# A six-layer cross network on one core: first rows and last blocks transposed on TensorE, first weights issued by ScalarE, last block finished in pieces

## The chip, the cores and the metric

The kernel runs on one core of one Trainium2 chip. The metric is device time in microseconds (us): the median of timed runs. Beside it stands one profiled execution, whose trace the profile is made from.

## The reference

A cross network: `x0` is 16384 x 1024, there are 6 layers with a 1024 x 1024 weight each, all in bfloat16.

```python
x = x0
for l in range(6):
    proj = jnp.einsum('bd,de->be', x, ws[l]) + bs[l]
    x = x0 * proj + x
return x
```

## The kernel before

**Tiling.** The 16384 rows are worked in 16 pairs (`pr`) of two blocks of 512 rows. All activations are held transposed: features on the 128 partitions, rows along the free dimension. `x0T[:, n, k, :]` is block n, feature group k of 8. Each layer of a pair is a 1024 x 1024 by 1024 x 1024 product, done as a seven-product (Strassen-like) scheme on 512 x 512 blocks: `pid` 1 to 7, each of 16 matmuls of 128 x 128 by 512 columns (`mm`, L241). In pairs 1 to 15 product 2 is split once more into smaller products of 256 columns (`inner`, L247). Products 1, 2 and 4 use blocks of the layer's weight as they are (W11, W21, W22); 5, 6, 7, 3 and 8 use combinations.

**Pair 0** also makes the combinations: `emit_combo` adds and subtracts weight blocks on VectorE (DVE), and `flush_saves` stores them in a scratch tensor `Lc` in HBM, from which pairs 1 to 15 load them. The first combination is product 5's, `w12 + W22`. The differences of activations (`T1` to `T4`, `Ops.t`) are made on DVE too; T1 needs both blocks of x0.

**After the matmuls** ScalarE (ACT) moves PSUM to SBUF with the bias (`abias`, L47) or without (`acopy`, L44), and DVE sums, multiplies by x0 (`f_mul`) and adds x (`f_add`). Both engines' operations are pinned to the order in which they are written (`pin`); TensorE's are not.

**Queues.** All DMAs are issued by SyncE (SP; its queue is written SPq), one after another. The weight ring `wring` holds 12 tiles of 512 KB; `prefetch_upto` issues loads ahead. At the start SP issues, in this order: W11 (L176), a DMA transpose of x0's rows 0 to 511 (L180), W21 (L182), a DMA transpose of rows 512 to 1023 (L184), W12 (L116, through `load_w12`), a DMA transpose of the biases (L187, cast to float on GpSimd at L190), W22 (L93), and then layer 1's loads.

**Between pairs** (shown for pair 0 to 1): the result `xst` is transposed back by one DMA transpose (L421) into `x0T`'s memory, stored (L424), and behind these stand the next loads from `Lc` (L93) and the transposes of the next x0 rows (L408).

**The last pair** has its result in four regions (feature half eh, block n). Each `f_add` of the last layer writes `xfin`, `out_region` issues a DMA transpose of that region (L210), and all four stores (L415) are kept behind the last of the transposes by `nosync`.

Of the kernel before, what the change touches and what calls it, by code (L numbers as in the profile page):

```python
# [6 lines left out]

ADD = mybir.AluOpType.add
SUB = mybir.AluOpType.subtract
# [7 lines left out]
def kernel(  # L17
# [22 lines left out]
    def vtt(out, in0, in1, op):  # L40
        return pin(nc.vector.tensor_tensor(out=out, in0=in0, in1=in1, op=op))  # L41
# [28 lines left out]
    def w_src(l, pid):  # L70
        wl = ws[l]
        if pid == 1:
            return wl[0:H, 0:H].rearrange("(k p) e -> p k e", p=P)
        if pid == 2:
            return wl[H:D, 0:H].rearrange("(k p) e -> p k e", p=P)
        if pid == 4:
            return wl[H:D, H:D].rearrange("(k p) e -> p k e", p=P)
        return Lc[l, CIDX[pid]].rearrange("p (k e) -> p k e", k=KH)
# [33 lines left out]
    def load_w12(l):  # L112
        st = combo_st.setdefault(l, {})
        if "w12" not in st:
            st["w12"] = w12_pool.tile([P, KH, H], BF16, name="w12")
            state["last_dma"] = nc.sync.dma_start(st["w12"][:], ws[l][0:H, H:D].rearrange("(k p) e -> p k e", p=P))  # L116
        return st["w12"]
# [54 lines left out]
            B, T = self.B, self.T  # L172
            return {1: B[0, 0], 2: B[1, 0], 3: B[1, 1]}[pid] if pid <= 3 else T[{4: 4, 5: 1, 6: 2, 7: 3}[pid]][:]

    wt0 = wring.tile([P, KH, H], BF16, name="wp")
    nc.sync.dma_start(wt0[:], w_src(0, 1))  # L176
    wtiles[(0, 0, 1)] = wt0
    x0T_next = x0t_pool.tile([P, 2, KD, NB], BF16, name="x0T")
    LK = L * KD
    nc.sync.dma_start_transpose(out=x0T_next[:, 0], in_=x0[0:NB, :])  # L180
    wt2 = wring.tile([P, KH, H], BF16, name="wp")
    nc.sync.dma_start(wt2[:], w_src(0, 2))  # L182
    wtiles[(0, 0, 2)] = wt2
    nc.sync.dma_start_transpose(out=x0T_next[:, 1], in_=x0[NB:2 * NB, :])  # L184
    load_w12(0)
    b_bf = const.tile([P, LK], BF16, name="b_bf")
    nc.sync.dma_start_transpose(out=b_bf[:], in_=bs.rearrange("l (m p) -> (l m) p", p=P))  # L187
    b_all = const.tile([P, LK], FP32, name="b_all")
    prefetch_upto(7)
    nc.gpsimd.tensor_copy(b_all[:], b_bf[:])  # L190
    ops = Ops(x0T_next, 0, False)
    ops.t(1)
    for pid in (5, 6, 3):
        emit_combo(0, pid)
    ops.t(2)
    emit_combo(0, 7)
    prefetch_upto(PREF)
    flush_saves()

    step = 0  # L200
    for pr in range(NPAIR):
        x0T = x0T_next
        xst = xst_pool.tile([P, 2, KD, NB], BF16, name="xst")
        last_pair = pr == NPAIR - 1
        xo_last = {"t": None, "regions": [], "tins": [], "xfin": None}

        def out_region(eh, n):
            if xo_last["t"] is None:
                xo_last["t"] = xo_pool.tile([P, 2, 2, KH, KH, P], BF16, name="xoS")
            ti_ = nc.sync.dma_start_transpose(out=xo_last["t"][:, eh, n].rearrange("p j k r -> p (j k) r"),  # L210
                                              in_=xo_last["xfin"][:, eh, n].rearrange("r j k p -> r (j k p)"))
            xo_last["regions"].append((eh, n))
            xo_last["tins"].append(ti_)

        for l in range(L):
            last_layer = l == L - 1
# [42 lines left out]
            def bank():  # L259
                return psX.tile([P, NB], FP32, name="px")  # L260
# [11 lines left out]
            def f_add(Cb, eh, r):  # L272
                n = r ^ flip
                c, xs = Cb[:, :, r, :], xsrc[:, n, eh * KH:(eh + 1) * KH, :]
                if last_pair and last_layer:
                    if xo_last["xfin"] is None:
                        xo_last["xfin"] = xst_pool.tile([P, 2, 2, KH, KH, P], BF16, name="xst")
                    v4 = lambda a: a.rearrange("r k (j p) -> r k j p", p=P)
                    vtt(xo_last["xfin"][:, eh, n].rearrange("r j k p -> r k j p"), v4(c), v4(xs), ADD)
                    out_region(eh, n)  # L280
                else:
                    vtt(xst[:, n, eh * KH:(eh + 1) * KH, :], c, xs, ADD)

# [3 lines left out]
            if small:  # L287
                w2i = weights(8)
                wi = w2i[:].rearrange("p k (j e) -> p k j e", e=HE)
                b = cur.rhs(2)  # L290
                ti = cur.ti
                EA = ei_pool.tile([P, KH, NB], BF16, name="ea")
                EB = ei_pool.tile([P, KH, NB], BF16, name="eb")
                c11, c12 = (slice(0, 2), slice(0, NQ)), (slice(0, 2), slice(NQ, NB))
                c21, c22 = (slice(2, 4), slice(0, NQ)), (slice(2, 4), slice(NQ, NB))
                q2, q5, q1 = bank(), bank(), bank()
                for m in range(3):
                    mm(1, w1, pA, m, True)
                    ev(P1s, pA, m, 0)
                inner(q1, w2[:, 0:2, 0:HE], b[:, 0:2, 0:NQ], True)  # L300
                evi(EA[:, c11[0], c11[1]], q1)
                inner(q5, wi[:, 0], ti[:, 0], True)
                evi(EB[:, c22[0], c22[1]], q5)
                mm(1, w1, pA, 3, True)
                ev(P1s, pA, 3, 0)
                inner(q2, w2[:, 2:4, 0:HE], b[:, 2:4, 0:NQ], True)
                evi(EB[:, c11[0], c11[1]], q2)
                pX = [bank() for _ in range(KH)]
                w5 = weights(5)
                mm(5, w5, pX, 0, True)  # L310
# [12 lines left out]
                evi(EA[:, c21[0], c21[1]], q1)  # L323
                w3 = weights(3)
                mm(3, w3, pX, 0, False)
                ev(S53, pX, 0, 0)
                mm(5, w5, pX, 3, True)
                ev(P5s, pX, 3)
                for m in range(1, KH):
                    mm(3, w3, pX, m, False)  # L330
                    ev(S53, pX, m, 0)
                half_sum(EA, EA, EB, 0)
                cur.t(3)
                vtt(EA[:, c22[0], c22[1]], EA[:, c22[0], c22[1]], EB[:, c22[0], c22[1]], ADD)
                cur.t(4)
                vtt(C1[:, :, 0, :], P1s[:], EA[:], ADD)
            else:
                P2s = evt()
                for m in range(KH):
                    mm(1, w1, pA, m, True)  # L340
                    ev(P1s, pA, m, 0)
                pX2 = [bank() for _ in range(KH)]
                for m in range(KH):
                    mm(2, w2, pX2, m, True)
                    ev(P2s, pX2, m)
                pX = [bank() for _ in range(KH)]
                w5 = weights(5)
                for m in range(KH):
                    mm(5, w5, pX, m, True)
                    ev(P5s, pX, m)  # L350
                w3 = weights(3)
                for m in range(KH):
                    mm(3, w3, pX, m, False)
                    ev(S53, pX, m, 0)
                cur.t(3)
                cur.t(4)
                vtt(C1[:, :, 0, :], P1s[:], P2s[:], ADD)
# [30 lines left out]
            if more:  # L388
                ops.inner_t((1,))
                ops.t(1)  # L390
                ops.inner_t((2, 3, 4))
            f_mul(C2, 1, 0)
            f_add(C2, 1, 0)
            if more:
                ops.t(2)
            if combos_next:
                emit_combo(l + 1, 7)
                emit_combo(l, 8)
                if l + 1 == L - 1:
                    stage_ctx.close()  # L400
                    xo_pool = ctx.enter_context(tc.tile_pool(name="xo", bufs=1))
            elif pr == 0:
                emit_combo(l, 8)
# [6 lines left out]
                        nosync(ti_, state["last_dma"], "keep the x0 prefetch behind the already issued weight loads")  # L410

        if last_pair:
            for (eh, n) in xo_last["regions"]:
                r0 = pr * PR + n * NB
                si = nc.sync.dma_start(out[r0:r0 + NB, eh * H:(eh + 1) * H].rearrange("(j p) d -> p j d", p=P),  # L415
                                       xo_last["t"][:, eh, n].rearrange("p j k r -> p j (k r)"))
                for ti_ in xo_last["tins"]:
                    nosync(si, ti_, "stores after all output transposes")
            continue
        xo = x0T[:].rearrange("p n k (j r) -> p (n k j) r", r=P)  # L420
        nc.sync.dma_start_transpose(out=xo, in_=xst[:].rearrange("r n k b -> r (n k b)"))  # L421
# [34 lines left out]
```

## Time and profile before

| | us |
|---|---|
| median of 3 runs | 2329.14 (2328.7 to 2329.48) |
| profiled execution, its own time | 2331.35 |
| its span, first to last instruction | 2329.6 |
| TensorE matmul busy in the span | 2295.6 (99%) |
| DVE busy | 1988.8 (85%) |
| ACT busy | 1824.4 (78%) |

Matmuls are pipelined and their busy time overlaps, so 99% does not mean that TensorE is at its peak. Lines such as L241 are lines of the kernel before. The changed kernel's lines are shifted: L41, L44 and L47 become L42, L45 and L48, L93, L107 and L116 become L94, L108 and L117, and L241 and L247 become L281 and L287.

### The profile page before, as it was taken

What the parts mean: (1) busy time and instruction counts of PE and PEld (TensorE: products, weight loads), DVE (VectorE), ACT (ScalarE), POOL (GpSimd) and SP (SyncE); (2) the same over time, 40 slices, a digit from 0 to 9 for tenths busy, and PEclk for the clock granted to TensorE, in tenths of its full rate; (3) what the DMA queues carried; (4) which work ended last, traced back from release to release, by engine and by line L of the source; (5) the groups of instructions that cost most, each with busy time, mean ns of one, the idle gap of its engine ahead of it and who ended that gap; (6) DMA issues with size and microseconds to landing.
All of it is one profiled execution on the core that took longest, in us unless ns stands there. A gap on an engine that the chain in (4) does not pass through costs nothing.

```text
span 2329.6 us, 31728 instructions
## 1 busy us (share of the span) xinstructions
PE 2295.6 (99%) x11832; PEld 1158.5 (50%) x11832; DVE 1988.8 (85%) x2220; ACT 1824.4 (78%) x2959; POOL 0.4 (0%) x5
## 2 busy tenths in 40 slices
PE   7999999999999999999999999999999999999997
PEld 3444454555545454555555454555555454545553
DVE  6997888888888888888888888888888888888886
ACT  4776787878878787878778787878878787878786
POOL 0000000000000000000000000000000000000000
PEclk9999999999999999999999999999999999999999
DMA  8759578595875958669596785957859588595854
GB/s 235 229 178 303 185 200 261 172 289 172 209 258 176 287 172 221 240 189 272 186 244 216 194 266 180 262 202 196 268 173 283 177 203 262 171 295 170 238 189 109
DMA packets 613833, 508.56 MB, mean 218 GB/s; under 512 B 399664, under 2 KB 552240, under 8 KB 613680
## 3 DMA queue, kind: packets, MB, share of 16 engines
q1 hardware_dynamic: 613680, 506.53, 73.6%
q8 instruction: 94, 1.54, 0.3%
q14 instruction: 59, 0.48, 0.1%
HBM read 390.07 MB, written 49.28 MB: 189 GB/s over the span
## 4 chain that ended last, share of the span: by engine, by line
PE 96%; DVE 2%; SPq 1%; DMA 1%; issue 0%; ACT 0%; DVEq 0%
PE px L241 84%; PE px L247 12%; DVE cb L41 1%; DVE wp L41 1%; DVE xst L41 0%; DMA wp<-Lc 0%; SPq L180 0%; DVE T L41 0%; DMA wp<-in_ws_dram 0%; SPq L184 0%; SPq L187 0%; ACT cb L47 0%; SPq L116 0%; SPq L182 0%; SPq L176 0%
## 5 line engine op out<-in xcount | busy, mean ns | idle before, releaser
L241 PEld LDWEIGHTS <-wp 128*128 128x128 bf16 x9312 | 911.9, 98 | 1022.7 <-issue 14.0
L241 PE MATMUL px<-T,wp 128*128 128x512 bf16 x6144 | 1405.0, 380 | 3.3 <-DVE wp L41 3.3
L47 ACT ACTIVATE ev<-px,b_all 128x512 bf16<-128x512 f32 x1152 | 791.3, 687 | 225.6 <-PE px L241 212.0
L241 PE MATMUL px<-xst,wp 128*128 128x512 bf16 x2640 | 620.9, 379 | 0.4 <-DVE xst L41 0.4
L44 ACT CAST ev<-px 128x512 bf16<-128x512 f32 x792 | 463.3, 585 | 179.1 <-PE px L241 166.8
L41 DVE TENSOR_TENSOR cb<-cb,x0T 128x2048 bf16<-128x2048 bf16 x384 | 469.7, 1223 | 10.0
L41 DVE TENSOR_TENSOR cb<-ev 128x1024 bf16<-128x1024 bf16 (+1 forms) x390 | 263.1, 696 | 232.1 <-ACT ev L44 232.1
L41 DVE TENSOR_TENSOR xst<-cb,xst 128x2048 bf16<-128x2048 bf16 x320 | 392.0, 1225 | 22.4 <-PE px L241 0.5
L47 ACT ACTIVATE cb<-px,b_all 128x512 bf16<-128x512 f32 x384 | 263.6, 687 | 67.9 <-PE px L241 54.8
L247 PEld LDWEIGHTS <-wp 128*128 128x128 bf16 x2520 | 246.7, 98 | 133.2 <-DMA wp<-Lc 5.4
L247 PE MATMUL px<-ti,wp 128*128 128x256 bf16 x1440 | 216.7, 273 | 5.0 <-DMA wp<-Lc 5.0
L44 ACT CAST ea<-px 128x512 bf16<-128x512 f32 x360 | 211.7, 588 | 0.0
L41 DVE TENSOR_TENSOR T<-xst,T 128x2048 bf16<-128x2048 bf16 x160 | 195.5, 1222 | 8.3
L41 DVE TENSOR_TENSOR T<-xst 128x2048 bf16<-128x2048 bf16 x160 | 194.9, 1218 | 0.0
L44 ACT CAST eb<-px 128x512 bf16<-128x512 f32 x270 | 160.2, 593 | 6.1 <-PE px L247 6.1
L241 PE MATMUL px<-x0T,wp 128*128 128x512 bf16 x528 | 126.5, 385 | 10.5 <-DMA x0T<-in_x_dram 10.5
L247 PE MATMUL px<-xst,wp 128*128 128x256 bf16 x900 | 136.1, 274 | 0.0
L41 DVE TENSOR_TENSOR ea<-ea,eb 128x1024 bf16<-128x1024 bf16 (+1 forms) x180 | 99.9, 555 | 28.6 <-ACT eb L44 28.6
L41 DVE TENSOR_TENSOR cb<-ev,ea 128x2048 bf16<-128x2048 bf16 x90 | 109.7, 1218 | 0.0
L41 DVE TENSOR_TENSOR xst<-cb,x0T 128x2048 bf16<-128x2048 bf16 x64 | 78.4, 1225 | 2.2
L41 DVE TENSOR_TENSOR ti<-xst 128x512 bf16<-128x512 bf16 x150 | 63.2, 422 | 4.0 <-PE px L241 0.5
L41 DVE TENSOR_TENSOR ti<-xst,ti 128x512 bf16<-128x512 bf16 x150 | 62.7, 418 | 0.0
(14 smaller groups left out, 170.4 us busy)
## 6 DMA issues: line engine op xcount, KB each, us to landing
wp<-Lc SPq DMA_DIRECT2D x450, 512.0 KB, 3.9
wp<-in_ws_dram SPq DMA_DIRECT2D x288, 512.0 KB, 4.6
out_dram<-x0T SPq DMA_DIRECT2D x30, 1024.0 KB, 9.9
Lc<-wp SPq DMA_DIRECT2D x30, 512.0 KB, 3.3
w<-in_ws_dram SPq DMA_DIRECT2D x6, 512.0 KB, 5.1
out_dram<-xoS SPq DMA_DIRECT2D x4, 512.0 KB, 4.8
x0T<-in_x_dram SPq DMA_TRANSPOSE x32, 7.8
x0T<-xst SPq DMA_TRANSPOSE x15, 12.2
```

Source lines behind the costliest of these rows:

```text
L41: return pin(nc.vector.tensor_tensor(out=out, in0=in0, in1=in1, op=op))
L44: return pin(nc.scalar.copy(out=out, in_=in_))
L47: return pin(nc.scalar.activation(out=out, in_=in_, func=IDENT, bias=bias, scale=1.0))
L241: nc.tensor.matmul(pts[m][:], lhsT=wt[:, k, m * P:(m + 1) * P], rhs=rhs[:, k, :], start=(start and k == 0), stop=(k == KH - 1), **kw)
L247: nc.tensor.matmul(pt[:, m * NQ:(m + 1) * NQ], lhsT=w[:, k, m * P:(m + 1) * P], rhs=rhs[:, k, :], start=(start and m == 0 and k == 0), sto ...
```

## The change

- **Start.** The DMA transpose of rows 0 to 511 is replaced: SP loads the rows as they lie, in two halves of the features (`xrows`), and TensorE transposes them, 128 x 128 at a time, by a matmul against an identity matrix (`transpose_rows`), four into one PSUM bank; ACT and DVE copy the banks in turn to `x0T`. The first half is transposed before product 1, the second after product 1's first column group. The identity is made on GpSimd (a memset, in the built program a reload of the code library, and a select). DVE's T1, the first combinations and their saves are emitted after the second half.
- The biases are loaded as rows and transposed by one matmul instead of a DMA transpose and a GpSimd cast.
- The four raw blocks of layer 0's weight are issued by ACT's queue, one of SP's DMAs standing between the others. SP's order becomes: first half of x0's rows, biases, second half, DMA transpose of rows 512 to 1023, layer 1's loads.
- Eight matmuls on zeros run on TensorE before the first transpose, and a one-column copy on ACT.
- **End.** Of the last pair's four regions the two of the first feature half (eh = 0) keep the DMA transpose, but each is stored at once. The two of the second half are transposed by TensorE (`out_pe`), copied out of PSUM by ACT, or by ACT and DVE in turn, and stored in two pieces each. The very last block's multiply and add on DVE are cut into parts of 2, 1 and 1 of its four feature groups. TensorE takes the last block's transposes part by part.
- Pairs 1 to 14, and the order of all instructions between start and end on ACT, DVE and SP, are as before.

```diff
+    zero = const.tile([P, NB], BF16, name="zero")
+    nc.vector.memset(zero[:], 0.0)
+    ident = const.tile([P, P], BF16, name="ident")
+    make_identity(nc, ident[:])
...
-    nc.sync.dma_start_transpose(out=x0T_next[:, 0], in_=x0[0:NB, :])
...
+    xrows = [ev_pool.tile([P, KH, NB], BF16, name="ev") for _ in range(2)]
+    raw = {i: wring.tile([P, KH, H], BF16, name="wp") for i in (1, 2, 4)}
+    combo_st[0] = {"w12": w12_pool.tile([P, KH, H], BF16, name="w12")}
+    for h in range(2):
+        pin(nc.sync.dma_start(xrows[h][:], x0[0:NB, h * H:(h + 1) * H].rearrange("(r p) d -> p r d", p=P)))
+        if h == 0:
+            pin(nc.scalar.dma_start(raw[1][:], w_src(0, 1)))
+            pin(nc.sync.dma_start(b_rows[:], bs.rearrange("l (m p) -> (l m) p", p=P)))
+    pin(nc.scalar.dma_start(raw[2][:], w_src(0, 2)))
+    pin(nc.sync.dma_start_transpose(out=x0T_next[:, 1], in_=x0[NB:2 * NB, :]))
+    pin(nc.scalar.dma_start(combo_st[0]["w12"][:], ws[0][0:H, H:D].rearrange("(k p) e -> p k e", p=P)))
+    pin(nc.scalar.dma_start(raw[4][:], w_src(0, 4)))
...
+    acopy(warm_in[:], zero[:, 0:1])
+    warm = ps[1].tile([P, NB], FP32, name="px")
+    for _ in range(8):
+        nc.tensor.matmul(warm[:], lhsT=zero[:, 0:P], rhs=zero[:], start=True, stop=True)
+
+    def transpose_rows(h):
+        for k in range(KH):
+            pt = ps[1].tile([P, NB], FP32, name="px")
+            for r in range(KH):
+                nc.tensor.matmul(pt[:, r * P:(r + 1) * P], lhsT=xrows[h][:, r, k * P:(k + 1) * P], rhs=ident[:],
+                                 start=(r == 0), stop=True, skip_group_check=True)
+            dst = x0T_next[:, 0, h * KH + k, :]
+            if k % 2 == 0:
+                acopy(dst, pt[:])
+            else:
+                pin(nc.vector.tensor_copy(out=dst, in_=pt[:]))
+
+    transpose_rows(0)
+    pb = ps[1].tile([P, NB], FP32, name="px")
+    nc.tensor.matmul(pb[:, 0:LK], lhsT=b_rows[:], rhs=ident[0:LK, 0:LK], start=True, stop=True)
+    pin(nc.vector.tensor_copy(out=b_all[:], in_=pb[:, 0:LK]))
...
+        def out_region(n):
...
+            pin(nc.sync.dma_start_transpose(out=xo_last["t"][:, n].rearrange("p j k r -> p (j k) r"),
+                                            in_=xo_last["xfin"][:, n].rearrange("r j k p -> r (j k p)")))
+            r0 = pr * PR + n * NB
+            pin(nc.sync.dma_start(out[r0:r0 + NB, 0:H].rearrange("(j p) d -> p j d", p=P),
+                                  xo_last["t"][:, n].rearrange("p j k r -> p j (k r)")))
+
+        def out_pe(pts, n, ms, yo):
+            for j in range(KH):
+                for m in ms:
+                    nc.tensor.matmul(pts[j][:, m * P:(m + 1) * P], lhsT=xst[:, n, KH + m, j * P:(j + 1) * P], rhs=ident[:],
+                                     start=(m == 0), stop=True, skip_group_check=True)
+                if ms[-1] != KH - 1:
+                    continue
+                if len(ms) == KH or j % 2 == 1:
+                    acopy(yo[:, j, :], pts[j][:])
+                else:
+                    pin(nc.vector.tensor_copy(out=yo[:, j, :], in_=pts[j][:]))
+                if j % 2 == 1:
+                    r0 = pr * PR + n * NB + (j - 1) * P
+                    pin(nc.sync.dma_start(out[r0:r0 + 2 * P, H:D].rearrange("(j p) d -> p j d", p=P), yo[:, j - 1:j + 1, :]))
...
                 for m in range(KH):
                     mm(1, w1, pA, m, True)
                     ev(P1s, pA, m, 0)
+                    if step == 1 and m == 0:
+                        transpose_rows(1)
+                        ops.t(1)
+                        for pid in (5, 6, 3):
+                            emit_combo(0, pid)
+                        ops.t(2)
+                        emit_combo(0, 7)
+                        flush_saves()
...
-            f_mul(C2, 1, 0)
-            f_add(C2, 1, 0)
             if more:
+                f_mul(C2, 1, 0)
+                f_add(C2, 1, 0)
                 ops.t(2)
+            else:
+                n1, n0 = 1 ^ flip, flip
+                pT = [bank() for _ in range(KH)]
+                out_pe(pT, n1, range(KH), evt())
...
+                parts = [slice(0, 2), slice(2, 3), slice(3, 4)]
+                vtt(c(parts[0]), c(parts[0]), xz(parts[0]), MULT)
+                vtt(c(parts[1]), c(parts[1]), xz(parts[1]), MULT)
+                vtt(xs(parts[0]), c(parts[0]), xs(parts[0]), ADD)
+                vtt(c(parts[2]), c(parts[2]), xz(parts[2]), MULT)
+                vtt(xs(parts[1]), c(parts[1]), xs(parts[1]), ADD)
+                vtt(xs(parts[2]), c(parts[2]), xs(parts[2]), ADD)
+                pT2 = [psA.tile([P, NB], FP32, name="px") for _ in range(KH)]
+                yo = evt()
+                out_pe(pT2, n0, (0, 1, 2), yo)
+                out_pe(pT2, n0, (3,), yo)
...
-                for ti_ in xo_last["tins"]:
-                    nosync(si, ti_, "stores after all output transposes")
```

More of the change, by code (lines that the diff above doesn't have):

```diff
@@ L6 @@
 from concourse._compat import with_exitstack
+from concourse.masks import make_identity
 ADD = mybir.AluOpType.add
@@ L173, in rhs @@
             return {1: B[0, 0], 2: B[1, 0], 3: B[1, 1]}[pid] if pid <= 3 else T[{4: 4, 5: 1, 6: 2, 7: 3}[pid]][:]
-    wt0 = wring.tile([P, KH, H], BF16, name="wp")
-    nc.sync.dma_start(wt0[:], w_src(0, 1))
-    wtiles[(0, 0, 1)] = wt0
-    x0T_next = x0t_pool.tile([P, 2, KD, NB], BF16, name="x0T")
[L179 to L188, printed above, removed]
+    LK = L * KD
+    zero = const.tile([P, NB], BF16, name="zero")
+    nc.vector.memset(zero[:], 0.0)
+    ident = const.tile([P, P], BF16, name="ident")
+    make_identity(nc, ident[:])
+    b_rows = const.tile([LK, P], BF16, name="b_rows")
@@ new lines @@
+    b_all = const.tile([P, LK], FP32, name="b_all")
+    x0T_next = x0t_pool.tile([P, 2, KD, NB], BF16, name="x0T")
+    xrows = [ev_pool.tile([P, KH, NB], BF16, name="ev") for _ in range(2)]
[6 more added lines that the diff above has]
+            pin(nc.sync.dma_start(b_rows[:], bs.rearrange("l (m p) -> (l m) p", p=P)))
@@ new lines @@
+    pin(nc.scalar.dma_start(raw[2][:], w_src(0, 2)))
+    pin(nc.sync.dma_start_transpose(out=x0T_next[:, 1], in_=x0[NB:2 * NB, :]))
+    pin(nc.scalar.dma_start(combo_st[0]["w12"][:], ws[0][0:H, H:D].rearrange("(k p) e -> p k e", p=P)))
+    pin(nc.scalar.dma_start(raw[4][:], w_src(0, 4)))
+    for i in raw:
+        wtiles[(0, 0, i)] = raw[i]
+    warm_in = const.tile([P, 1], BF16, name="warm_in")
+    acopy(warm_in[:], zero[:, 0:1])
+    warm = ps[1].tile([P, NB], FP32, name="px")
+    for _ in range(8):
+        nc.tensor.matmul(warm[:], lhsT=zero[:, 0:P], rhs=zero[:], start=True, stop=True)
@@ L189 @@
+    transpose_rows(0)
+    pb = ps[1].tile([P, NB], FP32, name="px")
+    nc.tensor.matmul(pb[:, 0:LK], lhsT=b_rows[:], rhs=ident[0:LK, 0:LK], start=True, stop=True)
+    pin(nc.vector.tensor_copy(out=b_all[:], in_=pb[:, 0:LK]))
     prefetch_upto(7)
-    nc.gpsimd.tensor_copy(b_all[:], b_bf[:])
     ops = Ops(x0T_next, 0, False)
[L192 to L196, printed above, removed]
     prefetch_upto(PREF)
-    flush_saves()
     step = 0
@@ L204 @@
         last_pair = pr == NPAIR - 1
-        xo_last = {"t": None, "regions": [], "tins": [], "xfin": None}
-        def out_region(eh, n):
+        xo_last = {"t": None, "xfin": None}
+        def out_region(n):
             if xo_last["t"] is None:
[L209 to L213, printed above, removed]
+                xo_last["t"] = xo_pool.tile([P, 2, KH, KH, P], BF16, name="xoS")
+            pin(nc.sync.dma_start_transpose(out=xo_last["t"][:, n].rearrange("p j k r -> p (j k) r"),
[17 more added lines that the diff above has]
+                    pin(nc.sync.dma_start(out[r0:r0 + 2 * P, H:D].rearrange("(j p) d -> p j d", p=P), yo[:, j - 1:j + 1, :]))
         for l in range(L):
@@ L274, in f_add @@
                 c, xs = Cb[:, :, r, :], xsrc[:, n, eh * KH:(eh + 1) * KH, :]
-                if last_pair and last_layer:
+                if last_pair and last_layer and eh == 0:
                     if xo_last["xfin"] is None:
-                        xo_last["xfin"] = xst_pool.tile([P, 2, 2, KH, KH, P], BF16, name="xst")
+                        xo_last["xfin"] = xst_pool.tile([P, 2, KH, KH, P], BF16, name="xst")
                     v4 = lambda a: a.rearrange("r k (j p) -> r k j p", p=P)
-                    vtt(xo_last["xfin"][:, eh, n].rearrange("r j k p -> r k j p"), v4(c), v4(xs), ADD)
-                    out_region(eh, n)
+                    vtt(xo_last["xfin"][:, n].rearrange("r j k p -> r k j p"), v4(c), v4(xs), ADD)
+                    out_region(n)
                 else:
@@ L391 @@
                 ops.inner_t((2, 3, 4))
-            f_mul(C2, 1, 0)
-            f_add(C2, 1, 0)
             if more:
+                f_mul(C2, 1, 0)
+                f_add(C2, 1, 0)
                 ops.t(2)
+            else:
+                n1, n0 = 1 ^ flip, flip
+                pT = [bank() for _ in range(KH)]
+                out_pe(pT, n1, range(KH), evt())
+                c = lambda ms: C2[:, ms, 0, :]
+                xs = lambda ms: xsrc[:, n0, KH:KD, :][:, ms, :]
+                xz = lambda ms: x0T[:, n0, KH:KD, :][:, ms, :]
+                parts = [slice(0, 2), slice(2, 3), slice(3, 4)]
[9 more added lines that the diff above has]
+                out_pe(pT2, n0, (3,), yo)
             if combos_next:
@@ L412 @@
         if last_pair:
[L413 to L416, printed above, removed]
-                for ti_ in xo_last["tins"]:
-                    nosync(si, ti_, "stores after all output transposes")
             continue
```

## The prediction

> **What bounds the kernel now.** I read the page's chain of work first, then that chain in order of time, then the windows by stage, then the timeline of both ends. By engine, the page's chain:
>
> ```profile
> PE 96%; DVE 2%; SPq 1%; DMA 1%; issue 0%; ACT 0%; DVEq 0%
> ```
>
> TensorE carries the end, and the change touches none of the matmuls of pairs 1 to 14. So only the stages where the chain leaves PE can pay. The chain in order of time, its first 24 us and the handoff from pair 0 to pair 1 (start, length, what):
>
> ```profile
> 1.25 7.23 SPq L180
> ...
> 9.15 5.33 SPq L184
> ...
> 16.34 5.68 DMA wp<-in_ws_dram
> ...
> 22.11 1.24 DVE wp L41
> ...
> 23.39 70.37 PE px L241 x312
> ...
> 189.02 8.95 DMA wp<-Lc
> ```
>
> SP is held 7.23 and 5.33 us by the issue of the two x0 transposes; W22 stands behind them, is issued at 16.34, and product 5's combined weight (W12 + W22) starts on DVE only at 22.11. The windows show what then runs (PE, PEld, DVE, ACT, POOL busy, then clock, DMA share, GB/s):
>
> ```profile
> 20.00:23.40 3.40, 0.06 (x2) 0.01 (x1) 1.25 (x2) 3.40 (x7) 0.00 (x0) 0.85 1.03 354
> 23.40:29.30 5.90, 5.90 (x15) 2.13 (x16) 5.87 (x6) 1.87 (x4) 0.00 (x0) 0.51 0.91 354
> 29.30:93.80 64.50, 64.50 (x300) 29.23 (x299) 62.47 (x65) 47.92 (x76) 0.00 (x0) 1.00 0.66 205
> 93.80:144.50 50.70, 50.27 (x233) 22.48 (x232) 49.41 (x52) 37.63 (x59) 0.00 (x0) 1.00 0.73 234
> ```
>
> PE idles 3.3 us, comes back at clock 0.51, and from 22.11 to 144.5 DVE works with hardly a gap (62.47 of 64.5, 49.41 of 50.7). Pair 0 is thus paced by when DVE starts its combinations; a start earlier by d moves all that follows by d. The tail, from the timeline:
>
> ```profile
> 2314.94 0.69 ACT L47 ACTIVATE cb<-px,b_all 128x512 bf16<-128x512 f32 x1 [0.18 <-PE px L241]
> 2315.66 1.23 DVE L41 TENSOR_TENSOR cb<-cb,x0T 128x2048 bf16<-128x2048 bf16 x1
> 2316.92 1.22 DVE L41 TENSOR_TENSOR xst<-cb,xst 128x2048 bf16<-128x2048 bf16 x1
> 2320.02 4.25 SPq L415 DMA_DIRECT2D out_dram<-xoS  x4
> ```
>
> PE's last matmul ends at 2314.92. After it come one eviction, two DVE operations, a transpose, four stores of which none is issued before 2320.02, and the landing of the last: 14.7 us without PE work.
>
> **The start, step by step.** SP now issues half of x0's first 512 rows, the biases, the other half, then one transpose; ScalarE issues W11, W21, W12, W22. At 0.45 to 0.58 us an issue (the plain weight loads' rows), ScalarE is through at about 2.8 and SP reaches its transpose at about 2.3 instead of 9.15. ScalarE's table load (1.28 us) and first copy stand behind its four issues and end by about 5, before PE has anything to evict: nothing. The weight loads moved past SP's transpose and the layer 1 loads behind it are not needed before 43: nothing.
>
> The Trainium skill, "DMA: Bandwidth & Descriptors", section "Issuing engines are not separate DMA queues", says that another issuing engine saves only the sequencer's issue time, usually small beside the transfer. It speaks against this edit. By it the four loads moved are worth four issues of some 0.5 us, and the start's gain would be nearer 2 us than the sum below. Here the two issues ahead of them held SP for 12.6 us, so page and row part over the word small, and the row decides.
>
> PE's first transpose waits for two things. The first x0 half: the first 512 KB load landed 4.8 us after its issue, with one competitor; again it has one (W11), so about 6. And the identity, made on GpSimd by a memset, a reload of the engine's code library, and a select. The memset and select are small (rows: 0.10 and 0.22 us for the memset and the cast). No row shows a reload; it is a fetch, and fetches issued in the first two microseconds took 4.8 us (L176) and 9.2 us (L180) to land, so from 0.3 us (none needed) to 13.6 us (the slowest landing of an x0 transpose). I take the middle of those two, 7 us: identity at 0.7 + 0.3 + 7 = 8.0. Call it t.
>
> The skill's "GPSIMD Engine Reference", section "Instruction dispatch", puts the first call of freshly loaded code at about 6 us; by that figure t would be 7.0 and the start no better, as the loads below then come last. No run here shows it yet.
>
> The eight matmuls on zeros run from about 1 to 4.5 (8 x 0.43, the cold spacing seen from 10.53 on). If t is 8, PE then idles 3.5 us, longer than the 3.3 us gap above after which the clock was 0.51: they buy nothing. 16 transposes of 128 columns: a quarter of 0.43 is 0.11 us each, the 256-column cold spacing (four in 0.86 from 198.02) is 0.21; I take 0.15, so 2.4 us. The last copy out of PSUM has no row on DVE; ScalarE's 128x512 cast is 0.59, DVE's 128x512 operation 0.42; with hand-over 0.7. Product 1's first column, four cold matmuls: the fourth starts at t + 3.8 and ends at t + 4.2. The second 16 transposes end at t + 6.6, their last copy at t + 7.3, T1 takes 1.22, and DVE starts the combined weight at t + 8.5 = 16.5. T1 also needs the transposed second half of x0 and the next step W22: 4.2 MB lie before them in all; at the 250 to 280 GB/s of the windows 10.5 to 20 that is 15.0 to 16.8 us after 0.7, so T1 starts at 15.7 to 17.5, and I take 16.3. The loads are a little later than PE's 15.3, and the combined weight starts at 17.5 instead of 22.1: **4.6 us**. Ends: with transposes at 0.11, t = 6 and the half of x0 landing 7.0 us after its issue (the fastest x0 transpose), about 8; with t = 13, 0.6.
>
> PE must not be later than that: transposes done at 14.6, 12 + 16 matmuls at 0.216 (warm by then: before, full clock came 5 us after 10.53) end at 20.7, product 5 at 24.1 against 29.86 before: 5.7 us. DVE's 4.6 counts. The bias path (cast on GpSimd after a landing at 18.7, for which ScalarE waited 5.4 us) also moves ahead and is covered. The added DVE copies (four of 0.6, one small) lie in time in which DVE idled before.
>
> **The tail, step by step.** The first two blocks' transposes and stores go out at 2305 and 2312, beside matmuls: covered. Block (1, n1) is added at 2315.59; 16 PE transposes at 0.11 (the warm spacing of the 256-column rows, four from 191.60 to 192.04; LDWEIGHTS 0.10) end at 2317.4, ScalarE's four copies at 2318.5, stores at about 2317.4 and 2318.6. The last block on DVE, from 2315.6: 0.69 + 0.42 + 0.69 + 0.42 + 0.42 + 0.42 (rows of 128x1024 and 128x512) with 0.02 to 0.04 between is 2318.8, 0.6 later than the whole operations. Its last four transposes end at 2319.3, two copies each on DVE and ScalarE at 2320.4, the last store is issued there. Landing 3.9 us (fastest of the four stores before; a piece is half as large, and the smallest transfer in the trace took 3.7) gives 2324.3, and the end 1.1 later as before, 2325.4 against 2329.6: **4.2 us**. Bounds: 3.0 if the pieces land in the median 4.8 and PE needs 0.15, 5.5 if they land in 2.6.
>
> Sum: 8.8 us. The profiled execution took 2331.35 (span 2329.6); it becomes 2322.55. The median of the runs is 2.2 lower: 2329.14 - 8.8 = **2320.3**.
>
> **Rivals.** (a) The identity or the loads come late, t = 13 or more: the start pays at most 0.6, the tail 4.2, time 2324.3, and 2327.3 at t = 16. For it: POOL did nothing of the kind before. Against: T1 waits for DMA until 16.3 anyway, which hides t up to 9.
>
> (b) Slower: GpSimd's code fetch queues behind the 4.2 MB of start loads (until 17.5 at the latest) and then takes the same 7: t = 24.5, DVE starts its combinations at 33.0, 10.9 later than now, the tail gives back 4.2: net +6.7, 2335.8. It decides from t = 17.8 on (17.8 + 8.5 - 22.1 = 4.2). Against: fetches do not wait for whole queues in this trace (W11 landed in 4.8 beside a transpose).
>
> (c) The handoff wait of 8.95 us at 189 (PE idle 4.95, then clock 0.67 to 206) changes. SP's order there is unchanged and its transposes of pair 0 follow DVE at 171.03, so it should move along whole. If it closed, 5 of idle and 2 of half clock would go as well, 2313; if SP's order slipped by the length of one of its issues there (5 to 6), it would grow to 2325 to 2326.
>
> (d) The tail's last store still waits on SP or on full DMA engines: tail 0, only the start's 4.6, 2324.5.
>
> **Chances.** Forecast 0.66 (own range 2315.5 to 2324); (a) 0.14; (b) 0.06; (c) 0.08, half each way; (d) 0.06. Range 2314.5 to 2326 leaves out (b), the late end of (a) and the good half of (c). This kernel's measurement tells about 0.2% (4.7 us) from no change. Faster than 2324.5: the forecast, half of (a) and (d), half of (c): 0.79. Within: 0.14. Slower: (b) and a remnant of (a): 0.07.
>
> **What would show it.** Right: the select on POOL ends near 8; the first combined weight starts near 17.5 on DVE; no half clock in product 5; the 8.95 us piece of the chain still there, 4 to 5 us earlier; the span ends 10 to 11 us after the last product matmul. Wrong: DVE's first T waiting past 18 for POOL or DMA, a wait for an eviction inside the transposes, or the handoff wait changed.

## The result, and the profile after

| | before | after |
|---|---|---|
| median, 6 runs each on one chip, us | 2329.31 (2328.65 to 2331.24) | 2319.58 (2318.61 to 2321.22) |
| ratio of the two | | 0.9958, 95% interval 0.9946 to 0.9971 |
| profiled execution, its own time, us | 2331.35 | 2319.24 |
| its span, us | 2329.6 | 2317.5 |

The change takes 9.7 us off the median: faster, by more than the 0.2% that the prediction gave as the least that can be told. 2320.3 was forecast, 2314.5 to 2326.0. The two profiled executions are 12.1 us apart, since that of before was 2.0 above its median; where those 2 us lay is seen below.

The page's chain of the kernel after, by engine:

```profile
PE 92%; DVE 6%; issue 1%; DMA 1%; ACT 0%; SPq 0%; DVEq 0%
```

The chain in order of time, from the start to the handoff (start, length, what):

```profile
2.25 13.99 DMA x0T<-in_x_dram
18.79 5.79 PE px L281 x26
...
139.47 7.28 PE px L281 x33
...
183.58 9.25 DMA wp<-Lc
```

The issue of transposes by SP is gone from the chain. What stands first is the landing of the one x0 transpose that is left. At 139.47 instead of 144.50 TensorE starts the second product of pair 0's sixth and last layer, the last point at which the chain of pair 0 leaves DVE. "Pair 0 ends" stands for this point from here on, in the expectations too, though that layer's matmuls run on to about 160. The handoff wait stands where it stood, 5.4 us earlier. DVE's share rises from 2% to 6% mostly because the chain runs through DVE from 31.93 on in pair 0, not only from 93.77 on as before.

The timeline of the first 23 us:

```profile
1.00 0.29 POOL masks.py:199 TENSOR_SCALAR_AFFINE_SELECT ident<-ident 128x128 bf16<-128x128 bf16 x1
...
2.25 11.88 SPq L193 DMA_TRANSPOSE x0T<-in_x_dram  x1
...
5.70 1.07 PE L208 MATMUL px<-ident,ev 128*128 128x128 bf16 x16 [0.92 <-DMA ev<-in_x_dram]
...
16.37 1.23 DVE L42 TENSOR_TENSOR T<-x0T 128x2048 bf16<-128x2048 bf16 x1 [4.03 <-DMA x0T<-in_x_dram]
...
17.51 1.22 DVE L42 TENSOR_TENSOR wp<-w,wp 128x2048 bf16<-128x2048 bf16 x1
```

The identity is ready at 1.29; PE's transposes wait for x0's first half, not for it. T1 waits 4.03 us for the DMA transpose of the other block, and product 5's combined weight starts at 17.51 instead of 22.11.

The timeline of the end, from the last eviction of a product:

```profile
2309.09 0.69 ACT L48 ACTIVATE cb<-px,b_all 128x512 bf16<-128x512 f32 x1 [0.18 <-PE px L281]
...
2311.39 3.00 SPq L253 DMA_DIRECT2D out_dram<-ev  x4
...
2311.40 1.40 PE L243 MATMUL px<-ident,xst 128*128 128x128 bf16 x16 [0.47 <-ACT ev L45]
2311.59 0.75 DVE L42 TENSOR_TENSOR xst<-cb,xst 128x512 bf16<-128x512 bf16 x2
```

The last add ends at 2312.34. SP has issued the last store 2.05 us later (2314.39) and the span ends 3.11 after that. Before, these two were 6.13 (2318.14 to 2324.27) and 5.33. From the last product matmul to the end of the span it is 8.43 us instead of 14.68.

### The profile page after: what moved, and what is told of

It reads as the page before. It is cut to its first block, busy times and chain, and to the rows that moved or that the text cites. A ratio compares the mean times of both kernels' runs of the same rounds, so it can differ in the third digit from the quotient of the medians.

```text
span 2317.5 us, 31676 instructions
## 1 busy us (share of the span) xinstructions
PE 2286.7 (99%) x11675; PEld 1161.2 (50%) x11905; DVE 1992.9 (86%) x2232; ACT 1830.7 (79%) x2970; POOL 0.7 (0%) x6
## 4 chain that ended last, share of the span: by engine, by line
PE 92%; DVE 6%; issue 1%; DMA 1%; ACT 0%; SPq 0%; DVEq 0%
PE px L281 80%; PE px L287 12%; DVE cb L42 2%; DVE xst L42 1%; DVE wp L42 1%; DVE T L42 1%; DMA x0T<-in_x_dram 1%; DMA wp<-Lc 0%; ACT ev L45 0%; DVE ti L42 0%; SPq L188 0%; DVE ev L250 0%; DVEq L42 0%; DVEq L511 0%; PE px L243 0%
## 5 line engine op out<-in xcount | busy, mean ns | idle before, releaser
L42 DVE TENSOR_TENSOR cb<-cb,x0T 128x2048 bf16<-128x2048 bf16 (+1 forms) x386 | 469.9, 1218 | 9.9
```

## The experiments

Times are medians beside the kernel before on the same chip (2329.4, 2329.56 and 2329.39 in the three timed groups); where there is one run (the late identities, the whole last block, the whole stores), the trace is what is read.

**The two halves apart.** The kernel before with only the changed start, and with only the changed end.

> The changed kernel's start with the tail of the kernel before. By the prediction's sum the start is worth 4.6 us; the trace of the changed kernel shows the last product 5.9 us earlier than the trace of the kernel before. So 4.6 to 5.9 us below the kernel before, with the first combined weight at 17.5 on DVE and 14.7 us from the last product matmul to the end. Rival: the two ends are not independent (a handoff or tail that moves with the start), and the gain lies outside 4 to 7 us.

> The kernel before's start with the changed kernel's tail (the identity is made on GpSimd at the start, with nothing waiting for it until the end). The prediction's sum for the tail is 4.2 us, the trace of the changed kernel shows 8.4 instead of 14.7 us after the last product matmul, so 6.2. Expected 4.2 to 6.3 us below the kernel before, and with the run of the start alone the two gains add to the whole change's 9.7 within 1.5 us. Rival (the tail's last store waits elsewhere): under 2 us.

Start alone: 2325.74, ratio 0.9983 (0.9974 to 0.9992), 3.7 us, less than the 4.6 to 5.9 expected. End alone: 2323.57, ratio 0.9975 (0.9965 to 0.9984), 5.8 us. The sum, 9.5, is the whole change's 9.7 within its error: nothing shows that the halves touch. The run with only the end has the old start, and so shows it a second time (its timeline):

```profile
1.25 4.94 SPq L183 DMA_TRANSPOSE x0T<-in_x_dram  x1
...
14.39 1.23 DVE L42 TENSOR_TENSOR T<-x0T 128x2048 bf16<-128x2048 bf16 x1 [14.39 <-DMA x0T<-in_x_dram]
...
20.59 1.23 DVE L42 TENSOR_TENSOR wp<-w,wp 128x2048 bf16<-128x2048 bf16 x1 [4.97 <-DMA wp<-in_ws_dram]
```

The first transpose held SP 4.94 us here, not 7.23, and the first combined weight started at 20.59, not 22.11 (20.78 in a third execution with the old start, that of the run with the stores at once further down). Pair 0 ended at 142.97 and 143.15 in these two, not at 144.50. The profiled execution of before had a late start: 1.3 to 1.5 of its 2.0 us above the median lie there.

**The weights on ScalarE's queue, alone and taken back.** First the kernel before with only that:

```diff
-    nc.sync.dma_start(wt0[:], w_src(0, 1))
+    pin(nc.scalar.dma_start(wt0[:], w_src(0, 1)))
 (the same for W21, W12, W22; both x0 transposes stay on SP)
```

> The kernel before, with one edit: layer 0's four raw weight blocks (W11, W21, W12, W22) are issued by ScalarE's queue; both blocks of x0 keep their DMA transposes on SP, the tail is as before. Theory L (the loads decide: DVE's chain of pair 0 starts when the transposed second block of x0 and W22 have landed, and what TensorE does before is covered): SP's two transposes start at 0.7 and about 8, the second lands at 16 to 17, the first combined weight starts on DVE at 17.5 to 18.5 instead of 22.1, and the time is 3.5 to 4.6 us below the kernel before. Theory P (the gain of the start needs TensorE's transposes, which let TensorE begin at 5.7 instead of 10.5 and run warm): product 1 begins no earlier than 10.5, and the time is within 1.5 us of the kernel before.

2329.11, ratio 1.0 (0.9991 to 1.0008): nothing. Its timeline:

```profile
0.74 8.97 SPq L180 DMA_TRANSPOSE x0T<-in_x_dram  x1
...
9.76 6.56 SPq L184 DMA_TRANSPOSE x0T<-in_x_dram  x1
...
18.47 1.23 DVE L41 TENSOR_TENSOR T<-x0T 128x2048 bf16<-128x2048 bf16 x1 [18.47 <-DMA x0T<-in_x_dram]
```

W22 is no longer late, but with four loads beside it the first transpose holds SP for 8.97 us, and T1 now waits for x0 until 18.47 instead of 14.39. One wait has taken the place of the other; the combined weight starts at 19.61, only 1.0 earlier than with the old start, and pair 0 ends at 142.54, 0.4 to 0.6 earlier. Then the changed kernel with the four weights back on SP:

```diff
-            pin(nc.scalar.dma_start(raw[1][:], w_src(0, 1)))
+            pin(nc.sync.dma_start(raw[1][:], w_src(0, 1)))
 (the same for W21, W12, W22, all ahead of the transpose)
```

> The changed kernel with the four raw weights of layer 0 back on SP's queue, all ahead of the one DMA transpose that is left; the transposes on TensorE and the whole tail stay. The Trainium skill, DMA: Bandwidth & Descriptors, Issuing engines are not separate DMA queues, has it that another issuing engine saves only issue time. Theory Q (the second queue is worth its issue time, and the start's gain comes from the transpose that left SP): the DMA transpose is issued four issues of 0.5 us later, at 4.3 instead of 2.25, holds SP as long or somewhat shorter since more bytes are then already moved, and lands 0 to 2 us later than 16.3; the first combined weight starts at 17.5 to 19.5, the time is 2319.5 to 2322. Theory A (ScalarE's queue is what lets the loads run beside the transpose): the start falls back by most of its 3.7 us, the first combined weight starts at 20 to 21, the time is 2322.5 to 2324.

2318.72, ratio 0.9955 (0.9942 to 0.9969), no slower than the change (0.9946 to 0.9971). Its timeline:

```profile
4.80 9.06 SPq L195 DMA_TRANSPOSE x0T<-in_x_dram  x1
...
15.99 1.23 DVE L42 TENSOR_TENSOR T<-x0T 128x2048 bf16<-128x2048 bf16 x1 [6.17 <-DMA x0T<-in_x_dram]
```

The transpose is issued 2.55 us later, holds SP 2.8 us less, and T1 starts 0.4 earlier. What pays at the start is that one of two DMA transposes of x0 is gone, not the second queue. (The new path of the biases was not run by itself.)

**Both blocks of x0 transposed on TensorE**, no DMA transpose at the start:

```diff
-    pin(nc.sync.dma_start_transpose(out=x0T_next[:, 1], in_=x0[NB:2 * NB, :]))
(in words:)
+    xrows: four half blocks, loaded as they lie; transpose_rows(1, 0) after m == 0 of
+    product 1, transpose_rows(0, 1) after m == 1, transpose_rows(1, 1) after m == 3;
+    ScalarE issues W11, W12, W22 and then W21
```

> The changed kernel, with the second block of x0 also loaded as rows and transposed on TensorE, so that SP issues no transpose at the start; W12 and W22 are issued before W21. Theory L: all start loads are plain (4.2 MB at the 350 GB/s that plain loads reach in the changed kernel's trace: 12 us), T1's data is there at 9 to 11, the first combined weight starts at 12 to 14.5 instead of 17.5, and the time is 2.5 to 5 us below the changed kernel, less what DVE's four additional copies of 0.65 us cost in its chain. Theory P: the start of DVE's chain is not what paces pair 0, or the additional transposes and copies cost as much as the loads give, and the time is within 1 us of the changed kernel.

2320.06, ratio 0.9959 (0.9946 to 0.9971): no better than the change. DVE's first combined weight starts earlier (timeline):

```profile
15.72 1.22 DVE L42 TENSOR_TENSOR wp<-w,wp 128x2048 bf16<-128x2048 bf16 x1
```

That is 1.8 us earlier than in the change, and yet pair 0 ends at 139.09, only 0.4 earlier. The windows say why (PE, PEld, DVE, ACT, POOL busy, then clock, DMA share, GB/s); first the change, then this run:

```profile
31.90:139.47 107.57, 104.97 (x475) 46.89 (x483) 104.83 (x110) 78.49 (x122) 0.00 (x0) 1.00 0.67 218
```

```profile
18.00:139.09 121.09, 121.03 (x560) 54.69 (x560) 118.21 (x122) 90.05 (x141) 0.00 (x0) 1.00 0.69 225
```

PE runs 560 matmuls of 0.216 us without a gap. In the change PE's waits for DVE in pair 0 come to 3.3 us (the view of waits: 2.0 and 1.3). That is all that an earlier DVE could still give, and here products 1 and 2, done later, eat it up.

**How late may the identity be?** The changed kernel with 28 and with 80 memsets of its tile ahead of it on GpSimd:

```diff
+    for _ in range(28):          # 80 in the other run
+        pin(nc.gpsimd.memset(ident[:], 0.0))
     make_identity(nc, ident[:])
```

> The changed kernel with 28 memsets of the identity's tile ahead of it on GpSimd, 0.26 us apart as the 80 were, so that the identity is ready at about 8.6: the prediction's t = 8, made real. Theory L (the landing of the transposed second half of x0 hides it): transposes and first column group at half pace until about 12.5, second transposes until about 14.5, T1 still at 16.4 for its DMA, the first combined weight at 17.5, pair 0 ends within 0.5 us of 139.5, time 2318.5 to 2321. By the run with the identity at 22.2, where the first combined weight came 7.2 us after it, the cover holds to t = 10.3. Rival E (PE's late products 1 and 2 count too, and there is no cover): product 5 starts 2 us or more later than 18.8, and pair 0 ends 2 us or more later.

> The changed kernel with 80 memsets of the identity's tile ahead of it on GpSimd, 0.20 us each, so that the identity is ready at about 16 to 17.5 instead of 1.3. Rival (a) of the prediction with t = 16: by its formula DVE's first combined weight starts at t + 8.5 = 24.5 to 26; with the durations of the changed kernel's trace (16 transposes 1.1 to 2.1 us, four matmuls 1.2 to 1.7, 16 transposes, copy 0.7, T1 1.2) at t + 5.5 to 8 = 21.5 to 25. Theory D (DVE paces pair 0): the end moves by as much as the first combined weight, 4 to 7.5 us. Theory E (PE paces it as well): products 1 and 2 are then still to be done, 28 matmuls of 0.216 behind the second transposes, product 5 starts at t + 10 to 12, 8 us or more later than the 18.8 of the changed kernel, and the end moves by those 8 or more.

With 28 (timeline):

```profile
8.33 0.29 POOL masks.py:199 TENSOR_SCALAR_AFFINE_SELECT ident<-ident 128x128 bf16<-128x128 bf16 x1
...
8.68 1.87 PE L210 MATMUL px<-ident,ev 128*128 128x128 bf16 x16 [3.90 <-POOL ident masks.py:199]
...
17.22 1.22 DVE L42 TENSOR_TENSOR wp<-w,wp 128x2048 bf16<-128x2048 bf16 x1
```

Identity at 8.62, combined weight at 17.22, pair 0 ends at 139.18, time 2319.64: hidden, as the prediction had it for t = 8. With 80 (timeline):

```profile
21.94 0.29 POOL masks.py:199 TENSOR_SCALAR_AFFINE_SELECT ident<-ident 128x128 bf16<-128x128 bf16 x1
...
29.42 1.22 DVE L42 TENSOR_TENSOR wp<-w,wp 128x2048 bf16<-128x2048 bf16 x1
```

The memsets came 0.26 us apart, not 0.20, so the identity was there at 22.23 and not at the 16 to 17.5 expected. The combined weight follows it by 7.2 us. It is 11.91 later than in the change, and pair 0 ends at 151.38, 11.91 later too: DVE's start sets the end, one for one, though product 5 starts 14.7 later on PE. The one run took 2331.51, as 2319.58 + 11.91 would have it. That is above the median of the kernel before (2329.56) but within its runs, which reach 2331.55; that it is slower is not shown. As estimates by t + 7.2, the cover holds to t = 10.3, and the whole gain of 9.7 would be spent at t = 20.0.

**The matmuls on zeros**, left out of the changed kernel:

```diff
-    warm = ps[1].tile([P, NB], FP32, name="px")
-    for _ in range(8):
-        nc.tensor.matmul(warm[:], lhsT=zero[:, 0:P], rhs=zero[:], start=True, stop=True)
```

> The changed kernel without the eight matmuls on zeros; all else as it is. Theory Z (they keep the clock, since they end at 4.8 and the first transpose starts at 5.7): without them the first 16 transposes and the four matmuls of product 1 run at half clock (2.1 us in place of 1.07, four matmuls at 0.43), but the second half of x0 lands only at 10.4, so that the first millisecond's order changes little: T1 still starts at 16.4 for its DMA, the first combined weight at 17.5; at most 12 matmuls of product 1 and 16 of product 2 run at half clock until about 11 and the end moves by 0 to 0.6 us. The prediction's word (they buy nothing, as the identity is late): no half clock more than with them, 0 us. Rival: the clock stays at half until 18 or beyond, PE is late for product 5 by 2 us or more, and the end moves by 2 us.

(By "first millisecond" the first microseconds are meant.) 2320.51, ratio 0.996 (0.9947 to 0.9972): nothing that can be told. The timeline:

```profile
5.79 1.89 PE L204 MATMUL px<-ident,ev 128*128 128x128 bf16 x16 [5.79 <-DMA ev<-in_x_dram]
...
17.38 1.22 DVE L42 TENSOR_TENSOR wp<-w,wp 128x2048 bf16<-128x2048 bf16 x1
```

The 16 transposes take 1.89 us instead of 1.07 without them, so the zeros do quicken PE. But x0's landing covers it; pair 0 ends at 139.35.

**The end: which part of it pays.** The kernel before, with the rule gone that holds all stores behind the last transpose (the third region's store still waits for the fourth transpose):

```diff
+            if len(xo_last["regions"]) == 3:
+                return
+            for (e_, n_) in xo_last["regions"][2 if eh else -1:]:
+                pin(nc.sync.dma_start(...))      # the region's store, as it was
...
-                for ti_ in xo_last["tins"]:
-                    nosync(si, ti_, "stores after all output transposes")
```

> The kernel before, with all four output transposes on DMA as they were; only the rule that no store is issued before the last transpose is gone: the first two regions are stored as soon as they are transposed, the last two behind the last transpose. Theory S (most of the tail's gain is that rule and the queue that it makes): last add 3.2 us after the last product matmul, transpose landed 4.3 us later, last store issued 0.8 later, landed 3 to 4 later: span ends 11.5 to 12.5 us after the last product matmul instead of 14.7, a gain of 2 to 3 us, about half of the tail's 5.8. Theory T (it is the transposes on TensorE that pay, the stores would wait for the last DMA transpose anyway): the gain is under 1 us.

2329.24, ratio 0.9998 (0.9989 to 1.0007). In its trace the span ends 13.7 us after the last product matmul, 1.0 less than before. Its timeline:

```profile
2314.83 5.30 SPq L210 DMA_TRANSPOSE xoS<-xst  x2
2315.11 1.23 DVE L41 TENSOR_TENSOR xst<-cb,xst 128x2048 bf16<-128x2048 bf16 x1
2320.28 2.76 SPq L218 DMA_DIRECT2D out_dram<-xoS  x2
```

From the last add (2316.34) to SP's last store it is still 6.7 us, because the last two transposes are issued one behind the other and the last store waits for the last to land. Only the landing of the stores is shorter (median 3.1 instead of 4.8 us). The trace fits theory T: the early stores alone bring 1.0 us of the 6.25. The times agree, but their interval leaves room for up to 2.6. That the transposes on TensorE bring the greater part follows from what is left; they were not run without the parts and the pieces. Then the changed kernel with the last block whole on DVE, and with each of the last two blocks stored in one piece of 512 KB:

```diff
-                vtt(c(parts[0]), c(parts[0]), xz(parts[0]), MULT)
 (and the other five parts)
+                f_mul(C2, 1, 0)
+                f_add(C2, 1, 0)
```

> The changed kernel with the very last block's multiply and add on DVE whole again (1.23 and 1.22 us) instead of in parts of 2, 1 and 1 groups; the transposes on TensorE and the stores in pieces stay. Theory by the steps: DVE ends 0.1 earlier (2.49 instead of 2.62), but no transpose can start before that, and 16 of them take 1.07 instead of the 4 that are left: the last copies come some 0.6 us later, the span ends 9.0 us after the last product matmul instead of 8.43. Rival: the parts buy nothing, since the four groups' transposes take less than the 0.23 us that the parts cost, and the tail stays within 0.2 us of 8.43.

```diff
-                if j % 2 == 1:
+                if j == KH - 1:
 (one store of the four groups)
```

> The changed kernel with each of the last two blocks stored in one piece of 512 KB after its four copies, instead of two of 256 KB. Theory by landings: the last store is issued at the same place (behind the last copy), and lands in 3.1 us, as the other 512 KB stores of the changed kernel's end, instead of 2.5: the span ends 9.0 us after the last product matmul instead of 8.43. Rival (the first block's whole store is queued into the last one's way, as the stores of the kernel before with 4.8 us): 9.8 to 10.8. Rival (bytes do not matter): 8.4.

With the block whole, the last product matmul ends at 2308.27 and the span at 2317.5: 9.2 us, 0.8 more than with the parts. DVE is done 3.23 us after the last product matmul, where it took 3.27 with the parts, but all 16 of PE's transposes then stand behind it:

```profile
2310.27 1.23 DVE L42 TENSOR_TENSOR xst<-cb,xst 128x2048 bf16<-128x2048 bf16 x1
...
2311.56 1.51 PE L243 MATMUL px<-ident,xst 128*128 128x128 bf16 x16 [1.43 <-ACT ev L45]
```

With whole stores it is 2308.58 to 2317.6: 9.0 us, 0.6 more. The landings by the DMA view, first whole, then in pieces (KB each, median us):

```profile
out_dram<-ev SPq DMA_DIRECT2D x2, 512.0 KB, 3.0
```

```profile
out_dram<-ev SPq DMA_DIRECT2D x4, 256.0 KB, 2.5
```

These are single traces and small terms: 0.8 and 0.6 us, where 0.6 was expected of each.

**The handoff wait, which the change leaves.** The changed kernel, with pair 0's two output stores behind three loads of layer 1 instead of ahead of all five:

```diff
+        if pr == 0:
+            held.append(store_pair)      # the two stores, emitted later
...
                 w5 = weights(5)
+                if held:
+                    held.pop()(behind=load_of[1, 1, 8])
```

> The changed kernel, with one thing more: pair 0's two output stores (2 MB, 5.93 us of issue on SP) are issued behind three of layer 1's loads from Lc instead of ahead of all five. Theory H (the handoff wait is SP's order, and the load only stands behind the stores): the load that PE waits for is issued at about 177.6 instead of 183.6, and lands in 3.3 to 7.3 us, ahead of 188 where PE wants it. PE's wait of 4.84 us and the lower clock behind it (mean 0.95 from 183.6 to 215, some 1.5 us) go, the time falls by 4 to 7 us to 2313 to 2316, as the prediction's rival (c) had it for a closed handoff. Rival R (the load waits for a free buffer of the weight ring, or full DMA engines make it slow): it is issued at 183 all the same or lands as late, and the wait stays within 1.5 us of what it is; time 2318 to 2320. Rival S (the stores and the next x0 transposes behind them come later and hold up layer 2's loads): a new wait after 205 and no gain, or a loss of up to 5.

2314.35 (2313.86 to 2314.6), ratio 0.9934 (0.992 to 0.9947): the fastest of all, some 5 us below the change; on the same chip the change without its matmuls on zeros took 2320.51. PE's wait in the change, by the timeline:

```profile
192.88 0.97 PE L287 MATMUL px<-ti,wp 128*128 128x256 bf16 x4 [4.84 <-DMA wp<-Lc]
```

SP's queue in the timeline, first of the change, then of this run:

```profile
177.56 5.93 SPq L484 DMA_DIRECT2D out_dram<-x0T  x2
183.58 7.32 SPq L94 DMA_DIRECT2D wp<-Lc  x5
```

```profile
177.12 1.93 SPq L96 DMA_DIRECT2D wp<-Lc  x3
179.15 8.66 SPq L490 DMA_DIRECT2D out_dram<-x0T  x2
187.85 5.16 SPq L96 DMA_DIRECT2D wp<-Lc  x2
```

The load that PE waited for did not wait for a buffer or for bandwidth; it stood behind 5.93 us of store issue. PE's wait of 4.84 us at 192.88 is gone (0.8 is left, at 212), and so is the lower clock behind it: the stretch from 183.58 to 215.00 has clock 1.00 instead of 0.95. Theory H holds. By the two ratios, from runs on different chips, the gain over the change is 0.24%.

## Why the prediction was right, and where it was not

The forecast was right, on two terms that erred in opposite ways: start 3.7 for 4.6, end 5.8 for 4.2. But for the identity and the queue (below), the path and the waits were as forecast; that the sum came within 0.7 us is in part luck.

- **First combined weight at 17.5:** 17.51, and set by the landing that was named, x0's transposed second block (T1 at 16.37; forecast 16.3). The mis-sized side is the old one: 22.1 was read from one execution, and two others with the same start show 20.59 and 20.78. Taken from these, DVE starts 3.1 to 3.3 earlier, and pair 0 ends 3.5 to 3.7 earlier, which is the 3.7 measured. The 0.4 between them is steady: from the combined weight to that end it is 122.4 us in all three traces with the old start, and 121.96 or 121.97 in the change, the start alone, and the runs with late identities, without zeros and with the weights on SP.
- **The identity at t = 8:** wrong by 6.7 us. No reload is seen, the select ends at 1.29. The Trainium skill's figure of about 6 us ("GPSIMD Engine Reference", "Instruction dispatch") does not show either. It cost the forecast nothing, since the cover was read rightly: an identity at 8.62 gave the same time. The sign that the prediction named, a select ending near 8, did not come. The formula t + 8.5 was t + 7.2.
- **Transposes of 0.15 us:** 1.07/16 = 0.067, against 0.12 (1.87/16) where PE comes from a longer idle time. Also covered.
- **The zeros buy nothing:** true of the time, for another reason. They do keep PE quick (1.07 for 1.89 us), but x0's second half lands at 10.40 with them and without.
- **The queue:** here the prediction set the row (SP held 12.6 us) over the Trainium skill's rule that another issuing engine saves only issue time ("DMA: Bandwidth & Descriptors", "Issuing engines are not separate DMA queues"). The step failed for this edit: moved alone, the weights gave 0.3 us, within the error, and taken back they cost nothing. The rule was the better guide; the row told of the transposes, and these had to be taken off the queue.
- **PE gains 5.7, DVE's gain counts:** right that DVE's counts. PE gained more than 5.7: product 5 ends at 22.42 where 24.1 was forecast, against 29.86. Pair 0 moved with DVE, here and with the late identity. How near PE is was not said, though the prediction's own row has it busy for 64.50 of 64.50 us: 3.3 us of waits are left in pair 0.
- **The end, 4.2:** in the traces 6.25. SP is through 2.05 us after the last add where the steps gave some 2 (2318.8 to the last issue at 2320.4 and its 0.4), so that term held. What was mis-sized is the landing, by 1.4: 3.9 us was the fastest of four old stores of 512 KB, issued together; 256 KB pieces took 2.5. The upper bound, 5.5, allowed for 2.6. The other 0.6 is DVE's parts: the steps put the last add 3.9 us behind the last product matmul (2314.92 to 2318.8), and it was 3.27. So the sign of 10 to 11 us to the end of the span did not come either: it was 8.43.
- **Rival (c), the handoff:** it moved along whole, 9.25 for 8.95. Its price of 7 if closed was near the mark: some 5.
- **Rival (b), slower:** with the identity forced to 22.2 the start falls back as described, and the one run is not faster than the kernel before. The turning point, estimated from it, is at about 20.0, not 17.8.
- **Between the ends:** from pair 0's end to the last product matmul the two traces part by another 0.8 us (5.03 against 5.85). 0.7 of it lies in the slow stretch behind the handoff wait, 8.15 us before (198.02 to 206.17) and 7.46 after (192.88 to 200.34). In the other traces with that wait the same stretch takes 7.1 to 8.5 us, with the old start (7.1 to 8.0) as with the new (7.2 to 8.5), so this part is not the change's.

## What to carry to other kernels

Read the stage that a sum rests on in more than one execution where it hangs on DMA landings: here one start was 1.5 us late, and the sum took that for gain. When a queue holds up a load, ask which of its entries is dear: moving cheap loads to another queue gave nothing, taking one DMA transpose off it brought the start's 3.7 us, and reordering two stores behind three loads gave 5. And price a cover by making the covered thing late on purpose; here a delay to 8.6 us cost nothing and one to 22.2 cost 11.9, and the two together place the edge near 10 better than one trace alone.

## What the runs showed of the hardware

- The time that the first x0 DMA transpose holds its queue was longer in the runs with more loads beside it: 4.94, 5.00 and 7.23 us in three executions with one weight load ahead of it, 8.97 with four loads beside it, 11.88 in the change, with two x0 halves and the weights. Issued 2.55 us later, it held SP 2.8 us less and landed no later.
- TensorE ran slowly after idling, with a granted clock of 1.00 in the record (in the kernel before, behind 3.3 us of idling, the record had 0.51): 16 transposes took 1.87 us after 3.9 and after 17.5 us of idling and 1.89 with no matmul before them, but 1.07 behind the matmuls on zeros; the four matmuls that follow took 1.89 against 1.19. The length of the idle time alone does not tell: the second 16 transposes took 1.65 us after 2.09 us of idling in the run with only the start, and 1.07 after 2.32 in the change.
- The first select on GpSimd took 0.29 us and began 0.07 us after the memset before it, with no loading of code to be seen.
